# Local queries and keys loaded as 18 consecutive tokens per partition, with block transposes that write with a step of 18

## The chip, the core and the metric

The kernel runs on one core of one Trainium2 chip. The metric is the device time of one execution in microseconds (us); the median of the runs shown counts.

## What is computed

An attention over `q`, `k`, `v` of shape (8, 8, 576, 64), that is 8 batches, 8 heads, 576 tokens, 64 values a head, followed by a bilinear feed-forward layer over 4608 tokens of 512 values:

```python
mask_local   = (rel >= 0) & (rel < 32)                      # heads 0 to 3; rel = query - key position
mask_strided = (rel >= 0) & (key % 32 == query % 32)        # heads 4 to 7
attn = softmax(where(mask, q @ k.T / 8, -1e9)) @ v
x = attn, heads side by side                                # (4608, 512)
out = ((x @ w_a) * (x @ w_b)) @ w_out                       # 512 -> 1536 -> 512
```

## The kernel before

The feed-forward layer goes through 9 token tiles of 512 tokens (t = 0 to 8). A tile has 16 slots: in each of slots 0 to 11, `ffn_ab` multiplies the tile by one block of 128 columns of `w_a` and one of `w_b` on TensorE (PE), line 581. Slots 12 to 15 multiply the products by `w_out`, in tiles 2 to 8 by a scheme of seven products (line 686) on sums that VectorE (DVE) forms in `fast_s` (lines 614 to 618), in tiles 0 and 1 plainly (line 768). In every slot of the first kind, ScalarE (ACT) copies the first result out of PSUM (line 598, `a_sb`) and DVE multiplies it by the second (line 601, or 603 in tiles 0 and 1), which writes `pf`. The results lie in four PSUM banks, so PE can start the second block of slot n + 2 only when DVE has finished the product of slot n.

Attention for batch b is interleaved by hand into tile b - 1: a dictionary says after which slot a score step `S0` to `S7` or a value step `V0` to `V7` stands. An `S` step is a set of score matmuls (line 385), the exponential on ACT (line 393) and a masking on DVE, a bitwise and of the probabilities with a mask (line 403). A `V` step is a set of value matmuls (line 486), logarithm and exponential of the sums on ACT (lines 495 and 496) and two DVE products (lines 500 or 502) that write the normalised result into `xT`, the input of the feed-forward layer.

The queries and keys must reach PE with the head values on the partitions. From the third batch on (b >= `FIRST_D` = 2) this takes three steps, which run during tile b - 2 (for b = 2 in tile 0 and the start of tile 1):

1. `load_qk`, called for the local heads (`strided` false) and for the strided ones, issues transfers on the queue of GpSimd (POOL), which also turn float32 into bf16. For local heads (line 212) one transfer brings one head of one tensor: partition 32h + y of tile `kl` or `ql` gets tokens y, y + 32, ..., 18 of them.
2. `step_D` transposes on DVE in blocks of 32 x 32. For local heads (line 327) each call handles half of the 18 groups, so a batch has two calls for keys and two for queries, each of 128 x 576 elements. The result `tk` or `tq` has the tokens in order. For strided heads (line 332, tiles `natk`, `natq`) there are three calls each.
3. Plain transfers on SyncE's queue (SP; lines 342 and 346) spread the result into `kT_buf` and `qz_buf`, where the score matmuls read it.

Which slot each of these is issued in is a list: `do(i, fn, ...)` puts a call behind slot i; g0 = 16(b - 2) is the first slot of tile b - 2. For b >= 4, head h's local loads stand at g0 + h - 2 (batch 3: g0 + h + 2), its strided loads at g0 + h + 2 (batch 3: g0 + h + 6), and the four local transposes at g0 + 3, 5, 7 and 9 (batch 3: 8, 9, 10, 11; batch 2: 14, 14, 15, 15, all loads of batch 2 at 0 and 1). Every engine works through its own list in program order. From slot 14 on, whenever calls stand behind a slot, POOL first does a cast or copy of one element (line 936, `pace`), which waits for that slot's last result, so that what follows on POOL is not issued before it. POOL also does two tensor subtractions of each of tiles 2 to 7 (line 881, from the calls `do(16 * t + 15, nc.gpsimd.tensor_tensor, ...)` and `do(16 * t + 17, ...)`), which stand behind the loads of the same slots.

Of the kernel before, what the change touches and what calls it, by code (L numbers as in the profile page):

```python
# [8 lines left out]
BF16 = mybir.dt.bfloat16  # L9
# [5 lines left out]
FIRST_D = 2  # L15
# [4 lines left out]
NY = 18  # L20
# [10 lines left out]
def kernel(  # L31
# [10 lines left out]
    nc = tc.nc  # L42
    B, H, S, D = q.shape
# [9 lines left out]
    HL = H // 2  # L53
# [4 lines left out]
    nat = ctx.enter_context(tc.tile_pool(name="nat", bufs=1))  # L58
# [120 lines left out]
    def blocks(nm, z):  # L179
        z = int(z)  # L180
        return sb.tile([128, 2, (S, RS * GP)[z]], BF16, tag=f"t{nm}{z}", name=f"t{nm}{z}", bufs=1)


    nats = {}
    shared = {}

    def load_qk(b, strided, heads=range(HL), names="kq"):
        for nm in names:
            src = {"k": k, "q": q}[nm]
            if b < FIRST_D:  # L190
                n, R, h0 = (NP, RS, HL) if strided else (96, RL, 0)
                w0 = {"k6": 0, "q6": 1536, "k8": 3072, "q8": 5120}[f"{nm}{R}"]
                if b not in shared:
                    shared[b] = nat.tile([128, FG * 5 * SW], BF16, tag="shared", name="shared")
                t = nats[b, nm, strided] = shared[b][:n, w0:w0 + HL * R * D].rearrange("p (h r d) -> p h r d", r=R, d=D)
                hs = slice(heads[0], heads[-1] + 1)
                nc.gpsimd.dma_start(out=t[:, hs], in_=src[b, h0:h0 + HL].rearrange("h (p r) d -> p h r d", r=R)[:, hs])  # L197
            elif strided:

                t = nat_s[nm]  # L200
                n = 32 if b == FIRST_D else YS
                for h in heads:
                    nc.gpsimd.dma_start(
                        out=t[32 * h:32 * h + n],
                        in_=bass.AP(tensor=src.tensor, offset=(b * H + HL + h) * S * D,
                                    ap=[[RS * D, n], [YS * RS * D, 3], [1, RS * D]]))
            else:
                if 0 in heads:
                    nats[b, nm, strided] = nat.tile([128, NY, D], BF16, tag=f"{nm}l", name=f"{nm}l")
                t = nats[b, nm, strided]  # L210
                for h in heads:
                    nc.gpsimd.dma_start(out=t[32 * h:32 * h + 32],  # L212
                                        in_=src[b, h].rearrange("(i y) d -> y i d", y=32))
            nats[b, nm, strided] = t

    def load_vl(b, blocks=(0, HL * 6)):
# [103 lines left out]
    def step_D(b, z, nm, part):  # L320
        src = nats[b, nm, z == 1]
        if part == 0:
            tl[b, z, nm] = blocks(nm, z)
        t = tl[b, z, nm]
        if z == 0:
            i = slice(NY // 2 * part, NY // 2 * (part + 1))
            nc.vector.transpose(t.rearrange("p h (i y) -> p i h y", i=NY)[:, i],
                                src[:, i].rearrange("p i (h d) -> p i h d", h=2))
            last = part == 1
        else:  # L330

            nc.vector.transpose(
                t.rearrange("p h (r c) -> p r h c", r=RS)[:, :, :, YS * part:YS * part + 32],
                src[:, part].rearrange("p (r h d) -> p r h d", r=RS, h=2))
            last = part == 2
        if last:
            for nm, c in {"k": (("k", 0),), "q": (("q", 0), ("k", 1), ("q", 1))}[nm]:
                t = tl[b, z, nm]
                for e in range(2):
                    if nm == "k":  # L340
                        dst = kT_buf[b % 2][z][64 * e:64 * e + 64, c]
                        nc.sync.dma_start(out=dst[:, PAD:] if z == 0 else dst[:, :RS * GP], in_=t[64 * c:64 * c + 64, e])
                        continue
                    for j in range(2):
                        r0 = 64 * c + 32 * j
                        nc.sync.dma_start(out=qz_buf[b % 2][j][z][64 * e + 32 * j:64 * e + 32 * j + 32, c],
                                          in_=t[r0:r0 + 32, e])
# [177 lines left out]
    def step_X(b, c):  # L525
# [22 lines left out]
    FN = {"Tk": step_Tk, "Tq": step_Tq, "S": step_S, "V": step_V, "X": step_X, "W": lambda b, n: fast_w(n, slice(0, 3)),  # L548
          "s": S_px, "m": S_m, "L": lead_vl, "Pk": lambda b, c: pair_up("k", c), "Pq": lambda b, c: pair_up("q", c),
          "Z": lambda b, n: zero_qz(0, nc.vector, ((1, 1),)), "D": lambda b, n: step_D(FIRST_D, 0, "k", n)}  # L550

    def run(b, slot):
# [244 lines left out]
    with tc.manual_schedule(engines={ENG.PE, ENG.SP, ENG.Pool, ENG.DVE, ENG.Activation}):  # L797
# [11 lines left out]
        for x, src in ((raw[0], k), (raw[1], q)):  # L809
            nc.sync.dma_start(out=x[:96].rearrange("p (h r d) -> p h r d", h=2, d=D),  # L810
                              in_=src[0, 0:2].rearrange("h (p r) d -> p h r d", r=RL))
        nc.sync.dma_start(out=raw[2][PAD:, :D], in_=v[0, 0, 0:LW, :])
        load_qk(0, False, (2, 3))
        load_qk(0, True, (0, 1), "k")
        select(ident, ALU.is_equal, 0, [[1, 128]], -1)
        spin(23)
        consts(0)
        zero_qz(1, nc.scalar, ((0, 1),))
        load_qk(0, True, (0, 1), "q")
        load_vl(0, (0, 12))  # L820
        mask_local()
# [6 lines left out]
        for nm in ORDER:  # L828
            if nm[0] == "*":
                spin(int(nm[1:]))  # L830
            elif nm == "C0":
                for x, cp, n in ((raw[0], nc.vector.tensor_copy, "k"), (raw[1], nc.scalar.copy, "q")):
                    t = nats[0, n, False][:, 0:2].rearrange("p h r d -> p (h r d)")
# [21 lines left out]
            elif nm[0] == "F":  # L855
                f = int(nm[1])
# [23 lines left out]
        def do(i, fn, *args):  # L880
            at.setdefault(i, []).append(lambda: fn(*args))
# [7 lines left out]
        for b in range(FIRST_D, B):  # L889
            g0 = 16 * (b - 2)  # L890
            if b == FIRST_D:
                do(0, load_qk, b, False)
                do(1, load_qk, b, True)
                do(16, load_vl, b)
                for h in range(HL):
                    do(20 + h, load_vs, b, (h,))
            else:
                for h in range(HL):
                    do(g0 + h + (2 if b == FIRST_D + 1 else -2), load_qk, b, False, (h,))
                    do(g0 + h + (6 if b == FIRST_D + 1 else 2), load_qk, b, True, (h,))  # L900
                    do(g0 + h + 10, load_vs, b, (h,))
                do(g0 + (10 if b == FIRST_D + 1 else 7), load_vl, b)
            gs = {2: (14, 14, 15, 15, 16, 16, 17, 17, 18, 18), 3: (8, 9, 10, 11, 12, 13, 14, 15, 16, 17)}.get(b) or (
                3, 5, 7, 9, 12, 13, 14, 15, 16, 17)
            for (z, nm, part), g in zip(((0, "k", 0), (0, "k", 1), (0, "q", 0), (0, "q", 1), (1, "k", 0), (1, "k", 1),
                                         (1, "k", 2), (1, "q", 0), (1, "q", 1), (1, "q", 2)), gs):
                if (b, z, nm, part) != (FIRST_D, 0, "k", 1):
                    do(g0 + g, step_D, b, z, nm, part)
# [61 lines left out]
```

## Time and profile before

| | us |
|---|---|
| median of 3 runs | 328.78 (328.57 to 328.88) |
| span of the profiled execution | 326.3 |
| PE busy | 320.6 (98%) |
| DVE busy | 265.7 (81%) |
| ACT busy | 202.7 (62%) |
| POOL busy | 177.2 (54%) |
| transposes of line 327, 24 together | 18.5 |
| issues of line 212 on POOL, 48 together | 32.1 |

The profile is of one execution. It gives its span, from the first to the last instruction, and no other time of that execution. A group's row reads: line, engine, operation, output <- inputs, shapes, count, then busy us and mean ns of one, then the idle time just before these instructions and what ended it. A row of the order in time reads: start, length, engine, line, instruction, count, and in brackets the idle time before it. Granted TensorE clock was 0.999 of full speed on average.

### The profile page before, as it was taken

What the parts mean: (1) busy time and instruction counts of PE and PEld (TensorE: products, weight loads), DVE (VectorE), ACT (ScalarE), POOL (GpSimd) and SP (SyncE); (2) the same over time, 40 slices, a digit from 0 to 9 for tenths busy, and PEclk for the clock granted to TensorE, in tenths of its full rate; (3) what the DMA queues carried; (4) which work ended last, traced back from release to release, by engine and by line L of the source; (5) the groups of instructions that cost most, each with busy time, mean ns of one, the idle gap of its engine ahead of it and who ended that gap; (6) DMA issues with size and microseconds to landing.
All of it is one profiled execution on the core that took longest, in us unless ns stands there. A gap on an engine that the chain in (4) does not pass through costs nothing.

```text
span 326.3 us, 7676 instructions
## 1 busy us (share of the span) xinstructions
PE 320.6 (98%) x2820; PEld 205.5 (63%) x2820; DVE 265.7 (81%) x509; ACT 202.7 (62%) x329; POOL 177.2 (54%) x295
## 2 busy tenths in 40 slices
PE   8999999999999999999999999999999999999995
PEld 6754655455555587557999985569555954584474
DVE  6766888889778999999999999999877845647562
ACT  6764775478778765777677757875677643313321
POOL 8935839599966655875577557853312031232021
PEclk9999999999999999999999999999999999999999
DMA  9999999999999798799979999898033022004004
GB/s 151 154 204 201 204 184 182 173 171 136 132 213 116 95 97 79 77 217 125 83 72 199 138 86 77 160 180 84 20 77 115 2 67 64 0 2 129 1 2 129
DMA packets 98869, 37.50 MB, mean 115 GB/s; under 512 B 76688, under 2 KB 96016, under 8 KB 98832
## 3 DMA queue, kind: packets, MB, share of 16 engines
q0 software_dynamic: 85968, 19.48, 64.5%
q1 hardware_dynamic: 12576, 17.34, 18.4%
q8 instruction: 22, 0.36, 0.4%
q10 hardware_dynamic: 288, 0.20, 0.2%
q14 instruction: 15, 0.12, 0.1%
HBM read 39.51 MB, written 9.44 MB: 150 GB/s over the span
## 4 chain that ended last, share of the span: by engine, by line
PE 96%; DMA 2%; POOL 0%; DVE 0%; issue 0%; POOLq 0%; ACT 0%; DVEq 0%
PE mm L581 56%; PE mm L686 17%; PE mm L768 6%; PE st L385 5%; PE o L486 4%; DMA shared<-in_q_dram 2%; PE mm L714 2%; PE o L442 1%; PE ab L581 1%; PE misc L154 1%; PE tp L511 1%; PE tp L296 1%; PE end L714 1%; PE tp L287 0%; POOL shared L197 0%
## 5 line engine op out<-in xcount | busy, mean ns | idle before, releaser
L581 PE MATMUL mm<-xT,wa_sb 128*128 128x512 bf16 (+1 forms) x472 | 110.3, 357 | 0.0
L581 PE MATMUL mm<-xT,wb_sb 128*128 128x512 bf16 (+1 forms) x472 | 110.3, 357 | 0.0
L598 ACT COPY a_sb<-mm 128x512 f32<-128x512 f32 x106 | 62.1, 586 | 48.3 <-PE mm L581 47.6
L936 POOL CAST pace<-pf 1x1 f32<-1x1 bf16 x84 | 31.4, 374 | 84.0 <-DVE pf L601 80.7
L581 PEld LDWEIGHTS <-wb_sb 128*128 128x128 bf16 x480 | 46.3, 98 | 44.0 <-issue 0.2
L601 DVE TENSOR_TENSOR pf<-a_sb,mm 128x512 bf16<-128x512 f32 x84 | 56.4, 672 | 17.0 <-PE mm L581 13.8
L581 PEld LDWEIGHTS <-wa_sb 128*128 128x128 bf16 x480 | 42.7, 98 | 31.3
L393 ACT ACTIVATE p<-st 128x576 bf16<-128x576 f32 (+1 forms) x64 | 41.6, 650 | 11.7 <-PE st L385 11.1
L495 ACT ACTIVATE xr<-o 64x576 f32<-64x576 f32 x48 | 31.1, 649 | 25.0 <-PE o L486 24.2
L686 PEld LDWEIGHTS <-ps 128*128 128x128 bf16 x360 | 34.6, 98 | 3.9
L496 ACT ACTIVATE xr<-xr 64x576 f32<-64x576 f32 x48 | 32.9, 685 | 1.5
L500 DVE TENSOR_TENSOR xT<-o,xr 64x288 bf16<-64x288 f32 x48 | 21.5, 447 | 7.2 <-ACT xr L496 6.7
L502 DVE TENSOR_TENSOR xT<-o,xr 64x288 bf16<-64x288 f32 x48 | 21.5, 448 | 6.2 <-ACT xr L496 5.1
L686 PE MATMUL mm<-wf,ps 128*128 128x256 bf16 x216 | 26.4, 273 | 0.0
L768 PE MATMUL mm<-wo_sb,pf 128*128 128x512 bf16 x96 | 23.4, 379 | 0.0
L403 DVE TENSOR_TENSOR p<-p,mask_l 128x576 int16<-128x576 int16 x32 | 22.2, 694 | 1.2 <-ACT p L393 1.1
L243 POOL DMA_DIRECT2D vs<-in_v_dram x24 | 19.7, 821 | 3.0 <-PE st L385 2.2
L212 POOL DMA_DIRECT2D kl<-in_k_dram x24 | 16.1, 671 | 5.5 <-issue 3.6
L212 POOL DMA_DIRECT2D ql<-in_q_dram x24 | 16.0, 666 | 5.2 <-DMA wo_sb<-in_moe_w_out_dram 3.8
L603 DVE TENSOR_TENSOR pf<-a_sb,mm 128x512 bf16<-128x512 f32 x22 | 14.9, 676 | 4.3 <-ACT a_sb L598 2.8
L936 POOL COPY pace<-y_sb 1x1 f32<-1x1 f32 x16 | 2.8, 177 | 27.8 <-ACT y_sb L669 15.1
L686 PE MATMUL mm<-wf,pf 128*128 128x256 bf16 x144 | 17.6, 273 | 0.0
(162 smaller groups left out, 502.1 us busy)
## 6 DMA issues: line engine op xcount, KB each, us to landing
out_dram<-y_sb SPq DMA_DIRECT2D x12, 512.0 KB, 4.6
out_dram<-y_sb SPq DMA_DIRECT2D x10, 256.0 KB, 3.3
vl<-in_v_dram POOLq DMA_DIRECT2D x6, 384.0 KB, 6.8
kl<-in_k_dram POOLq DMA_DIRECT2D x24, 72.0 KB, 3.0
ql<-in_q_dram POOLq DMA_DIRECT2D x24, 72.0 KB, 3.0
vs<-in_v_dram POOLq DMA_DIRECT2D x24, 72.0 KB, 3.7
wo_sb<-in_moe_w_out_dram POOLq DMA_DIRECT2D x4, 384.0 KB, 9.2
natk<-in_k_dram POOLq DMA_DIRECT2D x20, 72.0 KB, 3.3
```

The source lines that it names most:

```text
L212: nc.gpsimd.dma_start(out=t[32 * h:32 * h + 32], in_=src[b, h].rearrange("(i y) d -> y i d", y=32))
L393: nc.scalar.activation(p[:M, :, :W], st[:M, :, :W], ACT.Exp, scale=scale)
L403: nc.vector.tensor_tensor(pi, pi, mk, op=ALU.bitwise_and)
L495: nc.scalar.activation(r, sums, ACT.Ln)
L496: nc.scalar.activation(r, r, ACT.Exp, scale=-1.0)
L500: nc.vector.tensor_mul(dst[:, W * half:W * (half + 1)], o[:64, j, :W], r[:, j])
L581: nc.tensor.matmul(ps_[:, c0:c0 + n], lhsT=w[:, kk, 128 * f:128 * (f + 1)], rhs=xT[:, kk, x0:x0 + n], start=(kk == first and c0 == 0), sto ...
L598: nc.scalar.copy(a_sb, ab[0])
L601: nc.vector.tensor_mul(pf[:, f, :].rearrange("p (i a s) -> p a i s", i=2, s=16), halves(a_sb), halves(ab[1]))
L686: nc.tensor.matmul(bank[b][:, q], lhsT=lhs(g, q), rhs=rhs(g), start=new and q == 0 and g == 0, stop=g == FG - 1, skip_group_check=True)
L768: nc.tensor.matmul(ybank[j], lhsT=pf[:, f, 128 * j:128 * (j + 1)], rhs=wo_sb[:, f], start=(f == 0), stop=(f == FD - 1))
L936: nc.gpsimd.tensor_copy(pace, done)
```

## The change

For b >= 2 the local heads come in one transfer per tensor: partition p of `kl` or `ql` gets 18 consecutive tokens of the four heads in order (32 partitions a head). The block transposes then find, in block i, tokens i, i + 18, i + 36, ..., and write each of them to its place, so neighbouring results of a block lie 18 elements apart in `tk` and `tq`. For b >= 3 the calls move: keys at g0 - 1 and queries at g0 + 1 (batch 3: g0 + 3 and g0 + 5). The number and the shape of the transposes, their slots, the strided loads and all later steps stay.

```diff
             else:
-                if 0 in heads:
-                    nats[b, nm, strided] = nat.tile([128, NY, D], BF16, tag=f"{nm}l", name=f"{nm}l")
-                t = nats[b, nm, strided]
-                for h in heads:
-                    nc.gpsimd.dma_start(out=t[32 * h:32 * h + 32],
-                                        in_=src[b, h].rearrange("(i y) d -> y i d", y=32))
+                t = nat.tile([128, NY, D], BF16, tag=f"{nm}l", name=f"{nm}l")
+                nc.gpsimd.dma_start(out=t, in_=bass.AP(tensor=src.tensor, offset=b * H * S * D,
+                                                       ap=[[NY * D, 128], [1, NY * D]]).rearrange("p (i d) -> p i d", d=D))
             nats[b, nm, strided] = t
...
-            nc.vector.transpose(t.rearrange("p h (i y) -> p i h y", i=NY)[:, i],
+            nc.vector.transpose(t.rearrange("p h (y i) -> p i h y", i=NY)[:, i],
                                 src[:, i].rearrange("p i (h d) -> p i h d", h=2))
...
             else:
+                for n, nm in enumerate("kq"):
+                    do(g0 + 2 * n + (3 if b == FIRST_D + 1 else -1), load_qk, b, False, range(HL), nm)
                 for h in range(HL):
-                    do(g0 + h + (2 if b == FIRST_D + 1 else -2), load_qk, b, False, (h,))
                     do(g0 + h + (6 if b == FIRST_D + 1 else 2), load_qk, b, True, (h,))
                     do(g0 + h + 10, load_vs, b, (h,))
```

## The prediction

> **What bounds the kernel now.** I read the page first (busy shares, chain of waits), then busy time by stretches, then the order in time of VectorE (DVE) beside TensorE (PE), then the groups by shape, and last GpSimd (POOL) and the transfers.
>
> ```profile
> span 326.3 us, 7676 instructions
> ...
> PE 320.6 (98%) x2820; PEld 205.5 (63%) x2820; DVE 265.7 (81%) x509; ACT 202.7 (62%) x329; POOL 177.2 (54%) x295
> ...
> PE 96%; DMA 2%; POOL 0%; DVE 0%; issue 0%; POOLq 0%; ACT 0%; DVEq 0%
> ```
>
> PE is busy for 320.6 of 326.3 us and carries 96% of the chain. Its idle 5.7 us lie before 16 us and after 320 us, where the change touches nothing. So hardly anything can be gained; the question is whether something can newly make PE wait. In each row below, the columns are the stretch, its length, then busy us of PE, PEld, DVE, ACT, POOL, then granted clock, DMA share and GB/s.
>
> ```profile
> 90.00:100.00 10.00, 10.00 (x74) 5.13 (x72) 7.54 (x15) 7.48 (x13) 6.10 (x12) 1.00 1.36 191
> 140.00:150.00 10.00, 10.00 (x81) 5.27 (x80) 9.87 (x19) 7.99 (x13) 5.79 (x10) 1.00 1.20 203
> 230.00:240.00 10.00, 10.00 (x72) 5.28 (x71) 8.21 (x17) 7.78 (x13) 2.13 (x6) 1.00 0.14 34
> ```
>
> DVE's 81% is a mean of two regimes. From 110 to 230 us, where token tiles 2 to 5 run beside the loading of batches 4 to 7, it is 97 to 99% busy. All the transposes that the change touches run on DVE: the first two for batch 2 end tile 0, the others stand in tiles 1 to 5. Here is tile 3 on DVE (start, length, instruction):
>
> ```profile
> 127.66 2.25 DVE L403 TENSOR_TENSOR p<-p,mask_l 128x576 int16<-128x576 int16 x1
> ...
> 134.73 1.48 DVE L403 TENSOR_TENSOR p<-p,mask_l 128x576 int16<-128x576 int16 x1
> ...
> 137.67 0.78 DVE L327 STREAM_TRANSPOSE tk<-kl 128x576 bf16<-128x576 bf16 x1
> 138.37 0.65 DVE L601 TENSOR_TENSOR pf<-a_sb,mm 128x512 bf16<-128x512 f32 x1
> ...
> 154.86 1.18 DVE L616 TENSOR_TENSOR ps<-pf 128x2048 bf16<-128x2048 bf16 x1
> ```
>
> And PE at the places that need the last two:
>
> ```profile
> 139.14 1.03 PE L581 MATMUL mm<-xT,wb_sb 128*128 128x512 bf16 x4
> ...
> 155.96 1.80 PE L686 MATMUL mm<-wo_sb,ps 128*128 128x256 bf16 x15
> ```
>
> The product at 138.37 ends at 139.02 and frees the PSUM bank that PE fills at 139.14: 0.12 us to spare. L616 ends at 156.04; the third matmul of the group at 155.96, at 0.109 us each, needs its second half at 156.18: 0.14 us. PE does not wait, but DVE runs just ahead of where it would.
>
> **The change part by part.** *Transposes.* 24 instructions on L327, four for each of six batches, keep shape and count; only their writes change, from runs of 32 consecutive bf16 to single elements 36 bytes apart. Call what one gains X. No row shows DVE writing hundreds of single elements with such a hop, so X is bounded by the nearest rows:
>
> ```profile
> L502 DVE TENSOR_TENSOR xT<-o,xr 64x288 bf16<-64x288 f32 x48 | 21.5, 448 | 6.2 <-ACT xr L496 5.1
> L500 DVE TENSOR_TENSOR xT<-o,xr 64x288 bf16<-64x288 f32 x48 | 21.5, 447 | 7.2 <-ACT xr L496 6.7
> ...
> L327 DVE STREAM_TRANSPOSE tk<-kl 128x576 bf16<-128x576 bf16 x12 | 9.3, 775 | 0.8 <-DMA kl<-in_k_dram 0.6
> ...
> L307 DVE COPY kT0l<-tp 128x576 bf16<-128x576 bf16 x2 | 1.5, 758 | 0.9 <-PE tp L287 0.8
> ...
> L307 DVE COPY kT0s<-tp 128x576 bf16<-128x576 bf16 x2 | 0.9, 450 | 0.0
> ...
> L105 DVE MEMSET vs<- 72x32 bf16 x2 | 0.2, 85 | 0.1
> L106 DVE MEMSET vl<- 32x32 uint32 x2 | 0.2, 85 | 0.0
> ```
>
> - Low end, 0. L502 writes runs of four bf16 with gaps, L500 writes without gaps: 448 against 447 ns. L105 writes 32 single bf16 with a hop of 256 bytes in the time in which L106 writes 32 words on end. Below nothing is excluded: the transpose reads and writes as many elements as before.
> - A middle, 0.31 us: the L307 copies differ in reading 576 elements singly or on end, 758 against 450 ns.
> - High end, 0.59 us: one more step for every element. A step is 1.02 ns, from L603 (676 ns, 512 elements) and L500 (447 ns, 288): 229/224. Times 576.
>
> I take X = 0.45, midway between 0.31 and 0.59: L502's gaps leave pairs of words together and L105 writes only 32 elements, which a buffer may hide, so neither is a stream of single ones; L307's 576 singles are the nearest.
>
> The Trainium skill speaks against the change here. Its page "Vector Engine (DVE) Microarchitecture Reference", section 5.2 "Measured stream behaviour on trn2", says that a port keeps its full rate only while neighbouring elements come in runs of at least two adjacent 4-byte words, and gives 1.71 ns (a far hop on every write) to 2.50 ns (a step of 24 words) against 1.05; my estimate from that page is 0.38 to 0.84 us for X, and the sum below would be +4.4 to +15 us. L105 and L106 do not show such a penalty; no row has it at length.
>
> *What covers 4X in a batch.* In tile 2 DVE idles 0.36, 0.11 and 0.12 us between its first transpose (102.83) and L616, and L616 (120.84 to 122.02) leaves 0.14 us before the third matmul of PE's group of 121.94 (122.16). That covers about 0.7 us; the rest makes PE wait. In tiles 3 to 5 the idle time is smaller (0.5 to 0.8 us a tile in all), but there POOL gives something back:
>
> ```profile
> 126.98 0.66 POOL L212 DMA_DIRECT2D kl<-in_k_dram  x1 [0.30 <-issue]
> 127.63 0.66 POOL L212 DMA_DIRECT2D ql<-in_q_dram  x1
> 128.31 1.28 POOL L881 TENSOR_TENSOR y_sb<-ye,y_sb 128x512 f32<-128x512 f32 x1
> ```
>
> L403 takes 0.44 us everywhere but at the six places where it meets L881, as at 127.66 and 134.73 above: there it ends 0.32 us after L881 does, 1.0 to 1.8 us late. The change leaves one issue instead of two ahead of each L881, so each should end about 0.66 us sooner and DVE with it, 1.3 us a tile. It cannot be banked (DVE then waits for PE), but pays back the lag of up to 0.7 us carried over from the tile before. So each of batches 4 to 7 costs 4X - 0.7 = 1.1 us, together 4.4.
>
> Batch 2: after its fourth transpose (57.55) DVE idles 0.90 us; then no idle time until the product of 62.06, which ends 0.16 us before PE (62.90) needs its bank: 1.8 - 0.9 - 0.16 = 0.74. Batch 3: three transposes stand before the product of 81.97, which ends at 82.64; PE reads it in the sixth matmul of the group at 81.72, at 82.80: 3X - 0.16 = 1.19, less up to 0.57 if the first transpose, which waits 0.57 us for kl at 76.15, gets its data sooner: 0.9. Sum: 4.4 + 0.74 + 0.9 = 6.0 us.
>
> *Transfers.* 48 issues of 0.67 us become 12. By issues of other shapes (0.56 to 0.82 us) a new one costs about the same, so POOL sheds 36 x 0.67 = 24 us. Of 98869 packets, 48 x 576 = 27648 become 12 x 128 if a packet carries a partition's 18 tokens. Both are worth nothing directly: POOL idles 84 us in front of its pacing casts (L936), and the chain has DMA only at the start. A batch's keys are issued at g0 - 1 and its queries at g0 + 1 instead of by heads at g0 - 2 to g0 + 1 (batch 3: 19 and 21); behind them on POOL stand L881 (above) and the natk and natq issues, which the pacing holds in place. The first transpose now waits for one transfer of all heads.
>
> ```profile
> kl<-in_k_dram POOLq DMA_DIRECT2D x24, 72.0 KB, 3.0
> ...
> shared<-in_k_dram POOLq DMA_DIRECT2D x1, 288.0 KB, 8.8
> ```
>
> For 288 KB the rows give 8.8 us and more with the queue full, for 384 KB (vl) 6.2 to 7.4 us after 60 us. Tile 3: issue 126.98, first reader 137.67, so 10.7 us; queries 133.3 to 144.94. Batch 3 is nearest, 67.1 to 76.15. Cost 0 while it lands in time. On SP the issues behind a transpose move with it: S0 of tile 4 (160.16) needs the transfers issued until 155.24, which land in about 2.9 us: 2.0 us to spare against a lag of 0.7.
>
> **The rivals.**
> 1. *The hop is free; not slower.* For it: L502, L105. Then DVE only gains (L403), PE has nothing to take, and the time stays at 328.8 (328.4 to 329.4). It decides below X = 0.2, where 4 x (0.8 - 0.7) and some 0.2 for batch 3 stay under 0.66 us.
> 2. *More than one extra step.* At X = 0.59 the sum is 4 x 1.66 + 1.3 + 1.3 = 9.2 us, 338.0; at 0.72, 4 x 2.18 + 1.8 + 1.7 = 12.2, 341.0. For it: nothing covers it; against it: L502, L105.
> 3. *L881 does not move, or meets another DVE instruction.* Then tiles 3 to 5 pay the carried 0.7 us too: 3 x 0.7 = 2.1 more, 336.9.
> 4. *The load is late, or goes in 64-element pieces after all.* In pieces it is 2304 packets, with one issue's worth of time up to 4 x 0.67 us: PE sees nothing unless kl comes after its reader. If batch 3's comes in 11 us instead of 9, DVE and then PE lose up to 2 us; alone that is 330.8.
>
> **How the numbers follow.** The page gives the profiled execution's span, 326.3 us, and no other time of its own; the runs' median, 328.78, is 2.5 us above, which I take as what lies around the span. So 326.3 + 6.0 + 2.5 = 334.8. Chances: forecast (X from 0.2 to 0.6, rival 3 inside it) 0.47, rival 1 0.26, rival 2 0.24, rival 4 alone 0.03. 0.2% is 0.66 us, about what a measurement of this kernel can tell from no change. Slower 0.72, same 0.24, faster 0.04 (a hop that is free and a wait that this trace hides). The range runs from rival 1's low end to X = 0.72: 328.4 to 341.0. The forecast case alone spans 329.4 to 338.
>
> **What would show it.** Right: L327's mean over 1.1 us; DVE at 99% until 230 us; waits of PE for L601, L616 or L618 where there are none now; tiles 2 to 5 of 35 us instead of 34.0; L881 about 0.66 us sooner after its pacing copy. Wrong: L327 at 0.78 us, or at 1.1 us with tiles of 34.0 (cover I overlooked). PE waiting for DMA kl or ql would speak for rival 4; L327 above 1.4 us for rival 2.

## The result, and the profile after

The changed kernel takes 368.86 us (median of 4 runs, 367.28 to 369.91), the kernel before 328.83 us beside it (328.57 to 328.94): 1.1195 times as long, 95% interval 1.1137 to 1.1253. The prediction said slower, by 6 us; it is 40 us, far outside the range. One execution of a later run, the step alone, took 493.88 us at a mean granted clock of 0.657, against 0.977 to 0.991 in its other three, and is not counted.

In the changed kernel the lines from the loads on stand three lower: L327 is now L324, L403 L400, L581 L578, L601 L598, L603 L600, L616 L613, L686 L683, L881 L878. First the page of the changed kernel: the span, the busy shares, the chain of waits by engine, and the transfer of the keys (KB each, median us from issue to landing).

```profile
span 368.2 us, 7618 instructions
...
PE 332.4 (90%) x2820; PEld 206.7 (56%) x2820; DVE 302.6 (82%) x509; ACT 202.7 (55%) x329; POOL 152.8 (41%) x259
...
PE 70%; DVE 16%; issue 6%; ACT 3%; POOL 2%; DMA 2%; DVEq 0%; POOLq 0%
...
kl<-in_k_dram POOLq DMA_DIRECT2D x6, 288.0 KB, 4.4
```

PE, which carried 96% of the chain, now carries 70%, and DVE 16%. POOL sheds 24.4 us (177.2 to 152.8) and the load lands in 4.4 us, yet nothing of that shows in the time. DVE is busy 36.9 us longer. Its groups by shape say with what:

```profile
L324 DVE STREAM_TRANSPOSE tk<-kl 128x576 bf16<-128x576 bf16 x12 | 31.8, 2651 | 0.2
```

A transpose takes 2651 ns instead of 775 ns: X is 1.88 us by this row. A part of it is overlapped by the next instruction, as the order in time on DVE shows for the last of the four in tile 2 (start, length, instruction):

```profile
136.11 2.65 DVE L324 STREAM_TRANSPOSE tq<-ql 128x576 bf16<-128x576 bf16 x1
138.41 0.86 DVE L598 TENSOR_TENSOR pf<-a_sb,mm 128x512 bf16<-128x512 f32 x1
```

From the start of the transpose to the end of the product behind it are 3.16 us (139.27 less 136.11). Before, such a pair took 1.35 us (139.02 less 137.67, in tile 3). All pairs of tiles 2 to 5 lie within 0.02 us of these two. So what reaches the work behind is 1.81 us for each transpose, 43.4 us for 24. In the order in time on PE, the brackets give the idle time and what ended it:

```profile
128.16 1.02 PE L578 MATMUL mm<-xT,wb_sb 128*128 128x512 bf16 x4 [1.18 <-DVE pf L598]
133.74 1.02 PE L578 MATMUL mm<-xT,wb_sb 128*128 128x512 bf16 x4 [1.44 <-DVE pf L598]
...
139.33 2.16 PE L683 MATMUL mm<-wf,pf 128*128 128x256 bf16 x16 [1.77 <-DVE pf L598]
```

The first two are the PSUM bank that the product frees too late, the third is PE's sixth matmul on `w_out` waiting for the product of 138.41. The waits by releaser show how often it happens (total us, times, longest):

```profile
PE mm L578 <- DVE pf L598: 13.5, 12, 1.4
PE mm L683 <- DVE pf L598: 7.0, 4, 1.8
...
PEld L683 <- DVE ps L613: 1.4, 4, 0.3
```

Twelve, four and four: three waits for a bank, one for a product and one of the weight loads for the sums of L613 in each of tiles 2 to 5. In the stretch from 130 to 140 us (columns as in the prediction) PE is busy for 6.79 of 10 us and DVE for 9.91:

```profile
130.00:140.00 10.00, 6.79 (x57) 3.76 (x56) 9.91 (x13) 5.20 (x9) 3.12 (x4) 1.00 0.62 40
```

### The profile page after: what moved, and what is told of

The parts are those of the page before. It is cut to its first block, busy times and chain, and to the rows that moved or that the text cites. A ratio compares the mean times of both kernels' runs of the same rounds, so it can differ in the third digit from the quotient of the medians.

```text
span 368.2 us, 7618 instructions
## 1 busy us (share of the span) xinstructions
PE 332.4 (90%) x2820; PEld 206.7 (56%) x2820; DVE 302.6 (82%) x509; ACT 202.7 (55%) x329; POOL 152.8 (41%) x259
## 4 chain that ended last, share of the span: by engine, by line
PE 70%; DVE 16%; issue 6%; ACT 3%; POOL 2%; DMA 2%; DVEq 0%; POOLq 0%
PE mm L578 44%; PE mm L683 9%; DVE pf L598 5%; PE mm L765 4%; PE st L382 3%; PE o L483 3%; DMA vl<-in_v_dram 2%; ACT xr L492 2%; PE ab L578 2%; DVE ps L613 2%; DVE tk L324 2%; DVE xT L499 1%; PE mm L711 1%; DVE tq L324 1%; DVE p L400 1%
## 5 line engine op out<-in xcount | busy, mean ns | idle before, releaser
L578 PE MATMUL mm<-xT,wb_sb 128*128 128x512 bf16 (+1 forms) x472 | 111.0, 359 | 16.9 <-DVE pf L598 13.5
L578 PE MATMUL mm<-xT,wa_sb 128*128 128x512 bf16 (+1 forms) x472 | 111.0, 359 | 0.0
L578 PEld LDWEIGHTS <-wb_sb 128*128 128x128 bf16 x480 | 46.7, 99 | 64.3 <-issue 22.6
L598 DVE TENSOR_TENSOR pf<-a_sb,mm 128x512 bf16<-128x512 f32 x84 | 59.7, 711 | 17.0 <-PE mm L578 13.8
L578 PEld LDWEIGHTS <-wa_sb 128*128 128x128 bf16 x480 | 43.1, 99 | 32.2 <-issue 1.6
L683 PEld LDWEIGHTS <-ps 128*128 128x128 bf16 x360 | 34.3, 98 | 5.1 <-DVE ps L613 1.4
L324 DVE STREAM_TRANSPOSE tk<-kl 128x576 bf16<-128x576 bf16 x12 | 31.8, 2651 | 0.2
L324 DVE STREAM_TRANSPOSE tq<-ql 128x576 bf16<-128x576 bf16 x12 | 31.7, 2674 | 0.3
L497 DVE TENSOR_TENSOR xT<-o,xr 64x288 bf16<-64x288 f32 x48 | 21.7, 451 | 10.1 <-ACT xr L493 9.7
L765 PE MATMUL mm<-wo_sb,pf 128*128 128x512 bf16 x96 | 26.0, 409 | 2.0 <-DVE pf L600 2.0
L683 PE MATMUL mm<-wf,ps 128*128 128x256 bf16 x216 | 26.4, 273 | 0.0
L683 PE MATMUL mm<-wf,pf 128*128 128x256 bf16 x144 | 19.0, 273 | 7.3 <-DVE pf L598 7.0
L240 POOL DMA_DIRECT2D vs<-in_v_dram x24 | 19.7, 820 | 2.2 <-issue 1.9
L683 PEld LDWEIGHTS <-pf 128*128 128x128 bf16 x144 | 12.8, 98 | 11.0 <-DVE pf L598 9.5
L683 PE MATMUL mm<-wo_sb,ps 128*128 128x256 bf16 x144 | 18.2, 273 | 0.2
```

The costliest lines, as they stand in the source:

```text
L324: nc.vector.transpose(t.rearrange("p h (y i) -> p i h y", i=NY)[:, i], src[:, i].rearrange("p i (h d) -> p i h d", h=2))
L497: nc.vector.tensor_mul(dst[:, W * half:W * (half + 1)], o[:64, j, :W], r[:, j])
L578: nc.tensor.matmul(ps_[:, c0:c0 + n], lhsT=w[:, kk, 128 * f:128 * (f + 1)], rhs=xT[:, kk, x0:x0 + n], start=(kk == first and c0 == 0), sto ...
L598: nc.vector.tensor_mul(pf[:, f, :].rearrange("p (i a s) -> p a i s", i=2, s=16), halves(a_sb), halves(ab[1]))
L683: nc.tensor.matmul(bank[b][:, q], lhsT=lhs(g, q), rhs=rhs(g), start=new and q == 0 and g == 0, stop=g == FG - 1, skip_group_check=True)
L765: nc.tensor.matmul(ybank[j], lhsT=pf[:, f, 128 * j:128 * (j + 1)], rhs=wo_sb[:, f], start=(f == 0), stop=(f == FD - 1))
```

## The experiments

Six kernels ran. The theory after the result was that the write step alone costs the time, and that it does so because PE waits for DVE; the rivals are given in the expectations. To see where the time is lost, the table follows one and the same DVE instruction through the traces: each number is its start in that kernel's trace less its start in the trace of before. The columns are the first transpose of each batch (before: 54.8, 76.1, 102.8, 137.7, 171.4 and 205.6 us) and the last product of L601 (313.4 us). Differences in the text are taken before rounding.

| lag in us at | batch 2 | 3 | 4 | 5 | 6 | 7 | last product |
|---|---|---|---|---|---|---|---|
| the change | 2.9 | 8.6 | 16.8 | 22.3 | 29.0 | 35.1 | 41.9 |
| load alone | 0.0 | -0.6 | 0.1 | -0.8 | -0.4 | -0.4 | 0.1 |
| step alone | -0.1 | 5.4 | 12.2 | 19.7 | 27.9 | 34.5 | 41.3 |
| transposes twice | 1.0 | 2.5 | 5.4 | 7.7 | 10.8 | 13.4 | 16.2 |
| step for keys only | 0.1 | 1.8 | 5.3 | 7.2 | 10.3 | 12.8 | 16.0 |

Nearly all of the time is lost from the first of the transposes on. The 2.9 us ahead of it in the first row go with half the clock, which this one execution was granted from 17.3 to 24.1 us; in the trace of the load alone the lag there is 0.0. The 1.0 us of the transposes twice go with a wait of PE of 0.8 us at 23.1 us for a transfer of `wb_sb`. Without them the change lags by 39.0 us.

**The load alone.** The changed kernel, with writes on end:

```diff
-            nc.vector.transpose(t.rearrange("p h (y i) -> p i h y", i=NY)[:, i],
+            nc.vector.transpose(t.rearrange("p h (i y) -> p i h y", i=NY)[:, i],
```

> The new loads and their slots, with the transposes writing on end as before (so tokens stand in another order in the keys and queries; that part of the computation is changed). Theory (the write step of the transposes is the whole cost): transposes 0.78 us, time 328.8 us, within 0.7; 12 issues of 0.6 us on POOL; the masking that meets the POOL subtraction ends about 0.7 us sooner than before. Rival (the load of all heads comes late or its wait holds DVE up): above 332 us, with DVE waiting for kl or ql.

Measured: 328.62 us (median of 10), ratio 1.0001 (0.998 to 1.0022). Its masking instructions, in the answer on their line (ns min/median/max, first and last start), against up to 2255 ns before:

```profile
L400 DVE TENSOR_TENSOR p<-p,mask_l x32: 412/444/1244, 8.5 to 239.8; 128x576 int16<-128x576 int16 x32
```

So L881 does come sooner. Of the six masking instructions that met it (1.47 to 2.25 us long) three are now as short as the others, and three take 1.24 us; together the masking of the local heads takes 5.6 us less (22.2 to 16.6 us). DVE has 4.9 us less to do (265.7 to 260.8 us). PE, busy for 320.7 of 326.4 us, has nothing to take from it. The 24 us taken from POOL and the 26,700 packets fewer (98869 to some 72180) are worth nothing by themselves, as forecast.

**The step alone.** The kernel before, with the writes of the change:

```diff
-            nc.vector.transpose(t.rearrange("p h (i y) -> p i h y", i=NY)[:, i],
+            nc.vector.transpose(t.rearrange("p h (y i) -> p i h y", i=NY)[:, i],
```

> The loads and slots of before (tokens 32 apart, one transfer a head), with the transposes writing with a step of 18 (tokens land in another order; that part of the computation is changed). Theory: transposes 2.65 us and 368 us or up to 3 x 0.7 = 2 us more, since the POOL subtractions stay where they were. Rival (the loads carry part of the 40 us): clearly below, 350 to 364 us.

Measured: 370.45 us (median of three), ratio 1.1288 (1.1256 to 1.132). A transpose takes 2654 ns. The step is the whole cost, and without the new loads it costs a little more: from the first transpose on the lag grows by 41.4 us against 39.0. That the earlier L881 gives this back, once DVE is what PE waits for, fits but is not shown: no run moves L881 alone, and both traces have stretches of half clock, in different places. The runs agree in sign (the intervals of the two ratios just do not overlap), but the size of that difference is uncertain by about as much as it is.

**The transposes twice.** The kernel before, each of the 24 transposes issued a second time to the same place, on end, 0.70 us each:

```diff
             i = slice(NY // 2 * part, NY // 2 * (part + 1))
+            nc.vector.transpose(t.rearrange("p h (i y) -> p i h y", i=NY)[:, i],
+                                src[:, i].rearrange("p i (h d) -> p i h d", h=2))
             nc.vector.transpose(t.rearrange("p h (i y) -> p i h y", i=NY)[:, i],
```

> The kernel before, with every local transpose issued twice to the same place, both writing on end: 0.70 us more of DVE per transpose with no write step at all, so X = 0.70 in the sum of the prediction. Theory (only DVE time counts, and the cover is 0.7 us a batch in tiles 2 to 5): 4 x 2.1 + 1.7 + 1.6 = 11.7, 340.5 us, up to 2 more as the POOL subtractions do not move. Rival (long strided writes do something beyond the time on DVE, for instance to PE or the transfers, and plain DVE time is mostly covered): 329 to 335 us.

Measured: 344.56 us (343.76 to 344.89), ratio 1.0477 (1.0457 to 1.0496), 4 us above the sum of the expectation, 2 above its upper end. Of 16.8 us added to DVE, 15.2 stand in the lag from the first transpose on. No step is written here, so DVE's time as such is enough to make PE wait, and DVE has hardly any to spare. The expectation credited each of batches 4 to 7 with 0.7 us. By the lags batch 4 covers 0.5 of its 2.8 us, batches 5 to 7 together nothing, and batch 3 adds 2.9 us where 1.6 were expected.

**What a step costs.** Behind the last work of the kernel before, DVE and ACT instructions on 576 bf16 a partition, three of each, that differ only in the distance of what they write or read (`pin` is 576 elements on end, `fl` a tile with its columns in one row; "spaced" puts each block in a place of its own, with steps of 1, 2, 4, 6, 8, 9 and 10 elements, "inter" interleaves the blocks, with steps of 9 to 96):

```diff
+        for _ in range(3):  # spaced 4
+            nc.vector.transpose(fl(wa_sb)[:, :2304].rearrange("p (i h y s) -> p i h y s", h=2, y=32, s=4)[:, :, :, :, 0], pin)
...
+        for _ in range(3):  # inter 18
+            nc.vector.transpose(fl(wa_sb)[:, :1152].rearrange("p (h y i) -> p i h y", h=2, i=18)[:, :9], pin)
...
+            nc.scalar.copy(fl(wa_sb)[:, :576].rearrange("p (y i) -> p i y", i=18)[:, :18], fl(wb_sb)[:, :576].rearrange("p (i y) -> p i y", y=32))
```

> The kernel before, with probes on DVE behind its end, three of each: transposes of 128 x 576 with write steps from 1 to 96 elements (to 10 with each block in its own place, from 9 on with blocks interleaved), a copy with a write step of 18 and one with a read step of 18, a transpose that reads with a step of 18, and a copy on ACT that writes with a step of 18. Theory A (what costs is leaving a 16-byte line at each write): 0.78 us up to a step of 4, a rise up to 8, then flat at about 2.65; the copy that writes with a step of 18 costs about 3 ns an element more too. Theory B (single 2-byte writes cost, whatever the step): 2.65 already at a step of 2. Theory C (the steps fall on the same banks): 18 and some others dear, neighbours such as 16, 20 or 24 different by more than 0.3 us. The kernel's own time is longer by the probes, some 130 us.

The groups by shape, from the end of that kernel. In this order they are transposes with a write step of 1, 4, 6, 8 and 18 elements, a transpose that reads with a step of 18 and writes on end, and ACT's copy that writes with a step of 18:

```profile
L945 DVE STREAM_TRANSPOSE wa_sb<-wb_sb 128x576 bf16<-128x576 bf16 x3 | 2.3, 775 | 0.1
L949 DVE STREAM_TRANSPOSE wa_sb<-wb_sb 128x576 bf16<-128x576 bf16 x3 | 4.4, 1451 | 0.1
L951 DVE STREAM_TRANSPOSE wa_sb<-wb_sb 128x576 bf16<-128x576 bf16 x3 | 6.3, 2087 | 0.1
L953 DVE STREAM_TRANSPOSE wa_sb<-wb_sb 128x576 bf16<-128x576 bf16 x3 | 8.2, 2724 | 0.1
L967 DVE STREAM_TRANSPOSE wa_sb<-wb_sb 128x576 bf16<-128x576 bf16 x3 | 7.9, 2639 | 0.1
...
L987 DVE STREAM_TRANSPOSE wa_sb<-wb_sb 128x576 bf16<-128x576 bf16 x3 | 3.6, 1199 | 0.1
L989 ACT COPY wa_sb<-wb_sb 128x576 bf16<-128x576 bf16 x3 | 8.0, 2651 | 144.2 <-DVE wa_sb L987 144.2
```

With a step of 2 it is 820 ns. With steps of 2, 4, 6 and 8 elements the results lie in 144, 288, 432 and 576 pieces of 16 bytes, and each 144 more take 631 to 637 ns: 4.4 ns a piece. From 8 on every result has a piece of its own and the time stays (2579 to 2819 ns up to a step of 64; 3057 at 96). So the price goes with the pieces of 16 bytes, not with the distance. Expected was a flat price up to a step of 4 and the full one from 8; it rises from a step of 2 on. That a step of 18 might hit banks of memory that another step avoids is ruled out in this range: no step of 8 or more is cheap. The read side is far cheaper: 1199 ns, and 673 against 310 ns in a plain copy on DVE (1399 when the copy writes with the step). ACT's copy with the step takes what DVE's transpose takes. It was not run on end beside it; the nearest row, the copy of 128x576 bf16 out of PSUM on line 523 of the kernel before, takes 639 ns.

The Trainium skill says on its page "SBUF — State Buffer", section "Door 1: The DMA port swizzle", that the memory works in lines of 16 bytes, that two accesses to a line are enough for full bandwidth, and that bf16 may therefore be strided up to 8 elements. A price by pieces of 16 bytes is what is seen here; the rest is not, for writes of single bf16: with a step of 4, two to a line, the transpose already takes 1451 ns.

**Half the dose.** The changed kernel, with the step for the keys only:

```diff
-            nc.vector.transpose(t.rearrange("p h (y i) -> p i h y", i=NY)[:, i],
+            nc.vector.transpose(t.rearrange("p h (y i) -> p i h y" if nm == "k" else "p h (i y) -> p i h y", i=NY)[:, i],
```

> Half the dose: the changed kernel, but only the 12 key transposes write with a step of 18 (1.88 us more each, 22.6 us in all); the 12 query transposes write on end at 0.78 us (the queries' tokens stand permuted, which changes the values and no duration). Theory 'DVE is in front of PE in every tile': the sum per batch is 2 x 1.88 = 3.76 us less the cover of that batch: four times 3.76 - 0.7, batch 2 3.76 - 0.9 - 0.16, batch 3 3.76 - 0.46, together 18.2 us, so 328.8 + 18.2 = 347.0 us (346 to 349). Rival 'only the last transpose ahead of a product counts, the others have slack': well under half of the changed kernel's 40 us, 333 to 342 us. Rival 'part of the 40 us is the clock falling after long waits of PE, which a smaller dose would not set off': about 343 to 346 us with a granted clock of 0.99 or more.

Measured: 343.96 us (343.85 to 344.19), ratio 1.0459 (1.0438 to 1.048), at a granted clock of 1.0: 2 us below the first theory's lowest figure, within the third's. By the lag, 15.9 us of 12 x 1.81 = 21.7 show, so 5.8 are covered; at the full dose 43.4 - 39.0 = 4.4 are. The cover is about the same at both doses, as the first theory has it. Its expectation was too high because it used 1.88 for X (0.8 us) and too small a cover: 0.7 where batches 4 to 7 covered 0.4 to 1.7 (3.62 less the growth of 1.9, 3.1, 2.5 and 3.2), and 1.06 where batch 2 covered 1.9. The third theory has some part too: the changed kernel has two stretches of half clock in batches 2 and 3, 10.2 us together, this one none. PE is busy for 8.8 of those 10.2 us, so speed is lost in them, but part of it only takes the place of waiting for DVE. Batch 3, which holds 6.8 of them, adds 8.2 us to the lag; in the step alone, whose clock is full there, it adds 6.9. Batch 2 adds 5.7 and 5.5. That puts the clock's part in the 40 us at some 1.5 us, as an estimate from two traces.

**Singles, pairs and words.** Whether the price is one for each 16 bytes touched, or one for each write of less than a word of 4 bytes, the steps of bf16 leave open. Again behind the kernel before:

```diff
+            nc.vector.memset(fl(wa_sb)[:, :5760].rearrange("p (n s) -> p n s", s=10)[:, :, :1], 0.5)
...
+            nc.vector.tensor_copy(fl(wa_sb)[:, :2880].rearrange("p (n s) -> p n s", s=10)[:, :, :2], fl(wb_sb)[:, :576].rearrange("p (n s) -> p n s", s=2))
...
+            nc.vector.tensor_copy(fl(wa_sb)[:, :1728].rearrange("p (n s) -> p n s", s=12)[:, :, :4], fl(wb_sb)[:, :576].rearrange("p (n s) -> p n s", s=4))
...
+            nc.vector.tensor_copy(fl(wa_sb)[:, :2880].bitcast(mybir.dt.float32).rearrange("p (n s) -> p n s", s=5)[:, :, :1], fl(wb_sb)[:, :576].bitcast(mybir.dt.float32).rearrange("p (n s) -> p n s", s=1))
```

> The kernel before, and behind its last work VectorE instructions that write 576 bf16 (or fewer) with gaps, three times each; the time as a whole says nothing, only their rows. Theory 'a price for each 16-byte line that is opened' (4.4 ns with one port as in the transposes, 2.4 ns in a plain copy: 1399 ns / 576): memset of 576 singles 20 bytes apart 1.4 to 2.5 us; of 128 singles 0.31 to 0.56 us; of 32 singles 256 bytes apart 0.08 to 0.14 us, so that the 85 ns of the row L105 would have shown it only if set beside its 0.03 us of elements; copies: singles 20 bytes apart 1.40, pairs 20 bytes apart 288 x 2.43 = 0.70, pairs 8 bytes apart (two to a line) 0.35, runs of four 24 bytes apart 0.35, runs of eight 32 bytes apart 0.31, runs of sixteen 0.31; 288 float32 20 bytes apart 0.70, on end 0.31 or less; the addition of two tensors with singles 20 bytes apart 1.4 to 2.6 us. Rival 'a price for each write of less than 4 bytes' (a word has to be read before half of it is written): the same for the singles, but pairs and float32 20 bytes apart stay at 0.31 us.

The groups by shape: the addition with singles 20 bytes apart, then copies of singles 20 bytes apart, of pairs 20 bytes apart, of runs of four 24 bytes apart, and of 288 float32 20 bytes apart:

```profile
L954 DVE TENSOR_TENSOR wa_sb<-wb_sb 128x576 bf16<-128x576 bf16 x3 | 8.1, 2700 | 0.1
L956 DVE COPY wa_sb<-wb_sb 128x576 bf16<-128x576 bf16 x3 | 4.3, 1440 | 0.1
L958 DVE COPY wa_sb<-wb_sb 128x576 bf16<-128x576 bf16 x3 | 1.3, 425 | 0.1
L962 DVE COPY wa_sb<-wb_sb 128x576 bf16<-128x576 bf16 x3 | 0.9, 312 | 0.1
L970 DVE COPY wa_sb<-wb_sb 128x288 f32<-128x288 f32 x3 | 1.3, 427 | 0.1
```

The addition takes 457 ns on end, the copies 310. So every kind of instruction tried here pays for writing singles, not the transpose alone, while 4 bytes together cost at most 425 / 288 = 1.5 ns a piece. Neither theory holds as it stood: by pieces the pairs should have taken 0.70 us, by words 0.31 (and by words a step of 2 or 4 should have cost the transpose as much as a step of 8). What fits both probes is a price for each piece of 16 bytes that is high where less than a word is written at a time.

The memsets are the surprise. Their order in time, 576 on end (L944), 576 singles 20 bytes apart (L946), 32 singles 256 bytes apart (L948), 128 singles 80 bytes apart (L950):

```profile
324.62 0.54 DVE L944 MEMSET wa_sb<- 128x576 bf16 x1 [0.19 <-DVE wa_sb L944]
325.34 0.54 DVE L944 MEMSET wa_sb<- 128x576 bf16 x1 [0.19 <-DVE wa_sb L944]
328.01 0.54 DVE L946 MEMSET wa_sb<- 128x576 bf16 x1 [2.13 <-issue]
...
333.34 0.54 DVE L946 MEMSET wa_sb<- 128x576 bf16 x1 [2.13 <-issue]
334.06 0.09 DVE L948 MEMSET wa_sb<- 128x32 bf16 x1 [0.18 <-DVE wa_sb L946]
334.33 0.09 DVE L948 MEMSET wa_sb<- 128x32 bf16 x1 [0.18 <-DVE wa_sb L948]
...
335.87 0.17 DVE L950 MEMSET wa_sb<- 128x128 bf16 x1 [0.51 <-DVE wa_sb L950]
```

All of 576 have the same length, 0.54 us, but on end they follow each other after 0.72 us and with the gap after 2.67 us. The recorded length of a memset does not hold the price of the gaps; it stands as idle time in front of the row itself (2.13 us ahead of the first L946, which follows a memset on end, and 0.18 us behind the last). From start to start 32, 128 and 576 singles take 0.27, 0.68 and 2.67 us: 4.3 and 4.4 ns for each single more, the rate of the transposes. So 32 singles pay as well, 0.14 us by that rate, as an estimate, and their row of 0.09 us shows nothing of it.

## Why the prediction was wrong in size

**What bounds the kernel: right.** DVE stood just ahead of PE in tiles 2 to 5, and nearly all time added to it there makes PE wait; the three waits named came, four times each or more: for the bank (L578 for L598), for the product that PE's sixth matmul on `w_out` reads (L683 for L598) and, 0.3 us at a time, for L613, the L616 of before. In the trace of before none of them is there.

**X: the step that failed.** The term was taken as 0.45 us, between ends of 0 and 0.59, and it is 1.88 (1.81 for the work behind). The four rows that it was bounded by, one by one:

- L105 (85 ns for 32 singles, as for 32 words) was the argument for the low end. The last probe shows that this length could tell nothing: with a gap at each of 576 elements a memset is recorded as long as on end, and the price stands ahead of its row.
- L502 against L500 (runs of four bf16 with gaps, no dearer) is true, as 312 ns for runs of four against 310 on end shows. But four together are not singles.
- L307 against L307 (0.31 us) is a price of reading singles, there out of PSUM; in the probe, out of SBUF, it is 0.36 to 0.42 us. It was carried over to writing, which costs 1.88.
- One further step of 1.02 ns an element (0.59 us) was a guess at a mechanism that served as an upper end. Nothing in the trace capped the cost there; the addition that writes singles takes 2700 / 576 = 4.7 ns for each.

The nearest rows were not near: no row wrote more than 32 singles. The estimate from the Trainium skill's page "Vector Engine (DVE) Microarchitecture Reference", section 5.2, 0.38 to 0.84 us, has the right sign, and X is 2.2 times its upper end; the page's figures are for words of 4 bytes. The probe's float32 20 bytes apart (0.12 us more for 288, 0.4 ns each) show that in a plain copy words are far cheaper than single halves of them (1.13 us more for 576, 2.0 ns each).

**The cover: about right.** With X = 1.81 the prediction's own terms give 4 x (7.24 - 0.7) = 26.2 for batches 4 to 7, 7.24 - 0.9 - 0.16 = 6.2 for batch 2, and 3 x 1.81 - 0.16 - 0.3 = 5.0 for batch 3, together 37.4. The lags of the changed kernel give 25.1, 5.7 and 8.2, together 39.0; the medians differ by 40.0. Batch 3 was counted with three transposes since the fourth stands behind the product that PE waits for. The fourth counts too: in the trace of the step alone, where batch 3 adds 6.9 us, PE waits 1.34 us at 95.5 us for the value matmuls' input (L486 for L502), which DVE writes right behind the fourth transpose. Some 1.3 of the 8.2 us go with the half clock, by the comparison above (8.2 against 6.9).

A small term was off as well: the 2.5 us for what lies around the span. In the executions of the kernel before that have both a span and a time it is 2.1 to 2.2 us, in the changed kernel 1.7 to 1.8.

**L881 and rival 3.** After its pacing copy L881 came 0.73 us sooner at its first place in tile 3 (1.08 us after the start of the copy instead of 1.81) and 0.44 us at its second (1.09 instead of 1.53), against 0.66 expected. The masking is 1.9 us a tile shorter by it in the load alone (5.6 us over three tiles), against 1.3 expected. What that is worth to PE was not measured alone: the step alone is 1.6 us slower than the change in the medians, and its lag grows by 4.0 us more in batches 4 to 7, where it also has its two stretches of half clock. Rival 3, which priced the absence of the move at 2.1 us, had a size that fits and the case wrong.

**The other rivals.** Rival 1, a free hop, is out by the step alone. Rival 2 said the right thing, more than one extra step, and stopped at 0.72 us. Its own mark, L327 above 1.4 us, was passed by almost double. Rival 4 is out by the load alone: the time stays and the keys land in 4.7 us there (median; 4.4 in the change), below the 8.8 us of the row that the prediction went by.

## What to carry over

Price a strided write by what it writes at a time: here 576 single bf16, each in a 16-byte piece of its own, took 1.1 us (copy) to 2.2 us (addition) longer than on end on DVE and 1.9 us longer in the transpose, while pairs or runs of four with gaps cost 0.1 us or nothing. So a layout that saves a queue 26,700 small packets is no gain if it turns an engine's writes into singles. If a permutation must be paid somewhere, a strided read was far cheaper here (0.42 us in the transpose) than a strided write. And where no row shows the operation, the farthest rows are no ceiling: a row with few elements, or one whose length leaves the price out, can be right and still say nothing.

## What was not expected of the hardware

- A memset's recorded length leaves out what gaps in its writing cost: 538 ns with and without gaps, and with them 2.13 us of idle time in front of it.
- A plain copy on DVE pays about half as much for a single (1440 / 576 = 2.5 ns) as an addition or a transpose (4.6 to 4.7 ns). Why this is so was not tried.
- The granted clock, 0.999 on average before, has stretches of half speed in the changed kernel (3.4 us from 68.5, 6.8 us from 95.8) and in the step alone (3.4 us from 135.9 and from 176.9). Each of these begins 1.0 to 3.3 us after the start of a wait of PE of 2.0 to 3.4 us, but other waits as long (3.39 us at 62.5 and 2.20 at 257.6 us in the step alone) are followed by none, and the stretch of 6.8 us from 17.3 in the changed kernel follows no wait of PE above 0.9 us. So long waits of PE may cost speed on top; what decides it stays open.
